# A transformer block on one core: the attention outputs' scaling one step later, and the opening in another order

## The chip, the cores and the metric

The kernel runs on one core of a Trainium2 chip. The core has a matrix engine (PE, with its weight loads shown apart as PEld), a vector engine (DVE), a scalar engine (ACT), a third elementwise engine (POOL, GpSimd in the code) and queues that start DMAs (here nearly all on SP). Each engine works through its own list of instructions in the written order and waits on semaphores for the others. [...] The metric is the device time of one execution in microseconds; lower is better. Before the change it is 2756.73 us (median of 3 runs, 2753.68 to 2758.94).

## What is computed

One transformer block with adaptive layer norm, 2048 tokens of width 576, in float32:

```
mod = silu(c) @ w_mod                       # six vectors: shift, gain, gate for both halves
h = layernorm(x) * (1 + ca) + sa
q = h @ wq                                  # 32 heads of 128
p = softmax(q @ k^T / sqrt(128))            # k, v: the last 512 rows of a cache, 16 heads, each for 2 query heads
x = x + ga * ((p @ v) @ wo)
h = layernorm(x) * (1 + cb) + sb
x = x + gb * ((silu(h @ w1) * (h @ w3)) @ w2)   # inner width 4608
```

The inputs come from a fixed seed. The kernel keeps float32 accuracy with float16 matmuls: each operand is split into a high and a low half (`high = f16(a)`, `low = f16(a - high)`), and a product takes three matmuls, high by high, high by low and low by high.

## The kernel before

Tokens are worked on in four blocks of 512. The program has an opening (to about 60 us), attention (to about 1600 us) and the MLP.

**Attention** is a sequence of 128 slots, one for a query head and a block of tokens, each about 11.6 us long and cut in four steps, t = 0 to 3. Slots overlap like a pipeline: in slot i, PE computes the scores of slot i (`scores`, tile `pss`, one tile of 128 query rows a step), the query of slot i+1 (`query`, tile `pq`), the output projection of an older pair of heads (`attend_out`, tile `pe`, six matmuls a step), and at the slot's end the attention output of slot i-1 (`values`, tile `po`, twelve matmuls, weights `v`, moving operand `ptw`). DVE takes the maximum of each score tile (`table`, L487, and a small scaling, L488); ACT takes the exponential and the row sums (`p`, L500). The weights of tiles 0 to 2 are split by ACT and POOL (`hp`) and turned by DMA into `ptw`; the last tile (t = 3) is turned by PE one slot later, and its halves are made by ACT (`turn_high`, L527) at step 1 and by DVE (`turn_low`, L552, tile `ptw`) at step 2. DVE adds the projection to the running sum at steps 1 and 3 (`acc`, L592). Row sums are inverted on DVE (`l`), written to DRAM and read back to all partitions as `r` at the end of step 2 of slot i+1 (`sums`).

`normalize(i)` (L571) is a DVE instruction that multiplies `po` by `r` into a tile `on`; ACT and POOL split `on` at step 3 (`split_on`) for the projection. `on` shares its three buffers (tag "raw") with weight loads.

**PSUM.** All eight banks are in use: tags "A", "S" and "T" have two banks each, "E" is one tile of two banks. "A" goes to `pq` and `po` by turns, "S" to `pss`, "T" to turned tiles, "E" to `pe`.

The order of the work is written out by hand: the loop over slots and steps at the end of `tile_block` issues the instructions, and `at(i, t, task)` hangs other tasks (weight preparation, statistics, MLP weights) on a step; `run(i, t)` issues them. The scheduler keeps that order on every engine and adds waits where data or buffers need them.

**The opening** normalizes block 0, forms the modulation vectors (`weigh_col`, `mod_a`, `scale_first`), splits the first head's query weights (`put_in`, `split_in`: ACT scales and converts, POOL subtracts for the low half), makes `h` of block 0 (`modulate_first`, from the turned rows in PSUM) and the first query. Then the statistics of block 1 (`norm_stats`, `norm_root`, `norm_rows`) and its `h` (`make_h`, `modulate`, five parts m = 0 to 4) come in beside slots 0 and 1. `warm` issues matmuls without use for the result.

Of the kernel before, what the change touches and what calls it, by code (L numbers as in the profile page):

```python
# [14 lines left out]
AF = mybir.ActivationFunctionType  # L15
ALU = mybir.AluOpType
# [6 lines left out]
DC = 4  # L23
# [4 lines left out]
ST = SB // P  # L28
# [13 lines left out]
SCALE = float(DH) ** -0.5  # L42
P_LOG = 15 * math.log(2.0)
Q_DOWN = 2.0**-17
# [4 lines left out]
def tile_block(  # L49
# [14 lines left out]
    nc = tc.nc  # L64
# [36 lines left out]
    gate_down, score_down = sc[:, DC + 1 : DC + 2], sc[:, DC + 2 : DC + 3]  # L101
# [88 lines left out]
    def norm_stats(b, t):  # L190
        if t == 0:
            norms[b] = odd.tile([P, ST, 2], F32, tag="mv", name="mv"), {}
        st = odd.tile([P, 2, 6], F32, tag="bst", name="bst")
        for h in range(2):
            nc.vector.bn_stats(st[:, h, :], acc[b][:, t, h * HALF : (h + 1) * HALF])
        nc.vector.bn_aggr(norms[b][0][:, t, :], st.rearrange("p a b -> p (a b)"))
# [10 lines left out]
    def warm(ps, times):  # L207
        for _ in range(times):
            nc.tensor.matmul(ps[:, :P], ones, ident, start=True, stop=True)
# [26 lines left out]
    def turn_rows(b, m, tag):  # L236

        ps = t_bank() if tag == "T" else bank(tag, "ps_n")
        for t in range(ST):
            nc.tensor.transpose(ps[:, t * P : (t + 1) * P], norms[b][1][t][:, m * P : (m + 1) * P], ident)  # L240
        return ps

    def modulate(hT, m, ps, shift, gain, on_vector=False):

        g, s = gain[:, m : m + 1], shift[:, m : m + 1]
        hf = pool.tile([P, SB], F32, tag="hf", name="hf", bufs=HF)
        high = hT[:, m if m < DC else 2 * DC, :]
        if on_vector:
            nc.vector.tensor_scalar(hf, ps, g, s, op0=ALU.mult, op1=ALU.add)
        else:  # L250
            nc.scalar.activation(hf, ps, AF.Identity, bias=s, scale=g)
        nc.gpsimd.tensor_copy(high, hf)  # L252
        if m < DC:
            nc.gpsimd.tensor_sub(hT[:, DC + m, :], hf, high)
        else:
            nc.gpsimd.tensor_sub(high[DR:], hf[DR:], high[DR:])  # L256

    def modulate_first(hT, turned, shift, gain):

        def make(m, h):  # L260
            g, s = gain[:, m : m + 1], shift[:, m : m + 1]
            if m % 2:
                nc.vector.tensor_scalar(h, turned[m], g, s, op0=ALU.mult, op1=ALU.add)
            else:
                nc.scalar.activation(h, turned[m], AF.Identity, bias=s, scale=g)

        for m in range(DC + 1):
            make(m, hT[:, m if m < DC else 2 * DC, :])
        for m in (DC, 1, 0, 3, 2):
            tag, bufs = ("p", PB) if m < DC else ("hf", HF)  # L270
            h = pool.tile([P, SB], F32, tag=tag, name="hf", bufs=bufs)
            make(m, h)
            if m < DC:
                (nc.vector if m % 2 else nc.gpsimd).tensor_sub(hT[:, DC + m, :], h, hT[:, m, :])
            else:
                nc.gpsimd.tensor_sub(hT[DR:, 2 * DC, :], h[DR:], hT[DR:, 2 * DC, :])

# [57 lines left out]
    def up_of(g, k):  # L335
        return peaks[g][:, 10 + k : 11 + k]

    def split_in(raw, g, j):

        w = pool.tile([P, 2, DC + 1, P], F16, tag="w", name="wq", bufs=WB)  # L340
        nc.scalar.activation(raw, raw, AF.Copy, scale=up_of(g, j))
        nc.scalar.copy(w[:, 0], raw)
        nc.gpsimd.tensor_sub(w[:, 1], raw, w[:, 0])
        return w

    def load_out(g):

# [103 lines left out]
    n = len(slots)  # L451
    state = [dict() for _ in range(n)]
    hT, wqs, keys, vals, wos = {}, {}, {}, {}, {}
# [95 lines left out]
    def turn_low(i, t):  # L549
        cols = slice(t * P, (t + 1) * P)  # L550
        pt = state[i]["pt"]
        nc.vector.tensor_sub(pt[:, 1, :, cols], state[i]["t"], pt[:, 0, :, cols])  # L552
# [14 lines left out]
    def normalize(i):  # L567
        st = state[i]
        po = st.pop("po")
        on = st["on"] = pool.tile([P, SB], F32, tag="raw", name="on", bufs=RB)  # L570
        nc.vector.tensor_mul(  # L571
            on.rearrange("d (t p) -> d t p", t=ST),
            po.rearrange("d (t p) -> d t p", t=ST),
            st["r"].rearrange("d p t -> d t p"),
        )
# [470 lines left out]
    vecs, gates, tasks = {}, {}, {}  # L1046

    def at(i, t, task, *args):

        tasks.setdefault((i, t), []).append((task, args))  # L1050
# [32 lines left out]
    def scale_first(ps):  # L1083

        small = odd.tile([P, 16], F32, tag="us", name="us")
        nc.vector.tensor_scalar(mod_a[:, 1], mod_a[:, 1], 1.0, None, op0=ALU.add)
        nc.vector.tensor_reduce(small[:, 0:1], mod_a, axis=AX.XY, op=ALU.max, apply_absolute_value=True)
        spread = pool.tile([P, SB], F32, tag="kv", name="spread", bufs=8)
        nc.vector.tensor_scalar(spread[:, :P], ident, small[:, 0:1], None, op0=ALU.mult)
        nc.tensor.matmul(ps[:, :P], ones, spread[:, :P], start=True, stop=True)  # L1090
        nc.vector.tensor_reduce(small[:, 2:3], ps[:, :P], axis=AX.X, op=ALU.max)
        powers(small, small[:, 2:3], 0, 1, 5, 2.0**-9)
        nc.vector.tensor_scalar(mod_a, mod_a, small[:, 10:11], None, op0=ALU.mult)
        vecs["shift", "a"], vecs["gain", "a"] = mod_a[:, 0], mod_a[:, 1]
        nc.vector.tensor_scalar(score_down, small[:, 5:6], SCALE / Q_DOWN, None, op0=ALU.mult)

    def scale_gate(kind, small, to):

# [118 lines left out]
    def put_in(u, j):  # L1217
        wqs[u, j] = split_in(wqs[u, j], uses[u][0], j)
# [123 lines left out]
    for late in range(turns):  # L1342
        number = ITEMS + 4 * late
        loader, maker, w, _ = items[number]
# [35 lines left out]
    for d in range(2 * G):  # L1380
        g = 2 * d
# [19 lines left out]
    def begin_h(b):  # L1401
        hT[b] = new_h()

    def make_h(b, m, on_vector=False):
        modulate(hT[b], m, turn_rows(b, m, "T"), vecs["shift", "a"], vecs["gain", "a"], on_vector)

    def statistics(i, b, steps):
        for t in range(ST):
# [37 lines left out]
    for c in range(3):  # L1446
        i = 117 + 3 * c
# [19 lines left out]
    for c in range(3):  # L1467
        g = 12 + 6 * c
# [60 lines left out]
    warm(junk, WARM[0])  # L1529
    take_sums(0, 0, 3)  # L1530
    powers(peaks[0], peaks[0][:, 5:10], 0, 3, 5, 2.0**-14)
    put_in(0, 0)
    for m in (0, 1, 2, 3, 4):
        weigh_col(wms[1], 1, m, True)
    keys[0] = split_k(keys[0], 0)
    put_in(0, 1)
    scale_first(junk)
    warm(junk, WARM[1])
    begin_h(0)
    modulate_first(hT[0], turned, vecs["shift", "a"], vecs["gain", "a"])  # L1540
    score_factors(0)
    keys[0] = split_k_low(*keys[0], 0)
    for t in (0, 1):
        norm_stats(1, t)
    query(0, len(QP) - 1)
    for t in (2, 3):
        norm_stats(1, t)
    norm_root(1)
    at(0, 0, norm_scale, 1)
# [6 lines left out]
        at(0, t // 2, norm_rows, 1, t)  # L1556
    at(0, 2, begin_h, 1)
    for m in range(DC + 1):
        at(*((0, 2), (0, 3), (1, -1), (1, 0), (1, 1))[m], make_h, 1, m, m % 2 == 1)
    for d, step in enumerate((5, 6, 7, 4, 5)):  # L1560
        step_at(step, weigh, 2, d)

# [1 line left out]
    for i in range(n + 2):  # L1564
        run(i, -1)
        for t in range(ST):
            if t > 1 and i < n:
                turn_away(i, t - 2)
            if t == 0 and 1 <= i <= n:
                turn_away(i - 1, 2)  # L1570
            slot, tile = (i - 1 if t == 1 else n, ST - 1)
            if 0 <= slot < n:
                turn(slot, tile)
            if i < n:
                scores(i, t)
            if 2 <= i <= n and t == 1:
                normalize(i - 2)
            if 1 <= i <= n and t == 2:
                turn_low(i - 1, ST - 1)
                if i == n:  # L1580
                    turning.close()
                    after = ctx.enter_context(tc.tile_pool(name="after", bufs=1, space=PSUM))
                    lane[1] = (E, after.tile([P, 2, 512], F32, tag="T2", name="pf"))
            if t == 3 and i + 1 < n:
                query_low(i + 1)
            if i < n:
                weights(i, t)
            if t < 3 and i < n:
                half_high(i, t)
                half_low(i, t)  # L1590
            if t == 1 and 1 <= i <= n:
                turn_high(i - 1, ST - 1)
            if 1 <= i <= n and t < 2:
                sums(i - 1, t)
            if 2 <= i <= n and t == 3:
                split_on(i - 2)
            if i + 1 < n and t < ST - 1:
                query(i + 1, t)
            if i >= m0:
                for _ in range(3 if (i, t) == (n + 1, 0) else 1):  # L1600
                    next(stream)
            for piece in outs.get((i, t), ()):
                attend_out(*piece, (i, ("total", t)))
            run(i, ("total", t))
            run(i, ("taken", t))
            run(i, t)
            if 1 <= i <= n and t == 2:
                sums(i - 1, t)
            run(i, t)
        if 1 <= i <= n:  # L1610
            values(i - 1)
        if i == n:
            normalize(n - 1)
            split_on(n - 1)
# [73 lines left out]
```

## Time and profile before

| what | before |
|---|---|
| median of 3 runs | 2756.73 us (2753.68 to 2758.94) |
| the profiled execution: time, span of its instructions | 2758.39 us, 2756.2 us |
| PE busy | 2685.1 us, 97% of the span |
| DVE, ACT, POOL busy | 1997.3, 1617.8, 1881.1 us |
| mean granted clock of PE | 0.995 |

A row of a timeline gives the start in us from the span's start, the duration, the engine, the line, the operation, the tile written and the tiles read, shapes and types, how many were merged in the row, and in brackets the idle time of the engine before it and what ended it. A row of waits reads: who waited for whom, then us in total, times, longest us. A row of grouped instructions gives line, engine, operation, tiles, shapes and count, then busy us and mean ns of one, then the idle time before them and its enders.

### The profile page before, as it was taken

The page shows a single profiled execution, that of the slowest core. Times are in us where ns is not written, and L with a number is a line of the kernel's source. Part 1 is how long each engine was busy: PE and PEld are TensorE (multiplying, and loading weights), DVE is VectorE, ACT ScalarE, POOL GpSimd, SP SyncE. Part 2 cuts the span into 40 slices and gives each one's busy share as a digit, 9 for nine tenths or more (in the row PEclk, how much of TensorE's full clock was granted, in tenths as well). Part 3 has the DMA queues.
Part 4 walks back from the last instruction along what each step waited for, and adds up shares of the span by engine and source line. Part 5 has one row for each costly group of instructions (what it writes and reads, how often), then busy time and mean ns, then how long its engine had stood idle before and what let it go on. Part 6 is the DMA issues. An engine that isn't in the chain of part 4 may idle for free. (4 is left out here: it accounts for less than half of the span.)

```text
span 2756.2 us, 44751 instructions
## 1 busy us (share of the span) xinstructions
PE 2685.1 (97%) x15406; PEld 1512.8 (55%) x15406; DVE 1997.3 (72%) x3555; ACT 1617.8 (59%) x3013; POOL 1881.1 (68%) x1748
## 2 busy tenths in 40 slices
PE   6899999999999999999999999999999999999998
PEld 3455555555555555555555555555555555555555
DVE  7877788877788787877876667777766656666666
ACT  5777778777777877777677735544443333333332
POOL 5577788888788977877669637688873465333435
PEclk8999999999999999999999999999999999999999
DMA  5778888778786887989889945656643444333332
GB/s 186 171 178 193 194 182 188 175 176 189 169 185 166 190 196 180 214 181 210 192 189 208 256 131 171 200 167 200 210 149 108 161 121 128 103 102 111 104 107 87
DMA packets 593460, 463.84 MB, mean 168 GB/s; under 512 B 442704, under 2 KB 472528, under 8 KB 592208
## 3 DMA queue, kind: packets, MB, share of 16 engines
q1 hardware_dynamic: 592944, 460.69, 65.5%
q8 instruction: 121, 1.98, 0.3%
q14 instruction: 107, 0.88, 0.1%
q10 hardware_dynamic: 288, 0.30, 0.0%
HBM read 264.19 MB, written 95.99 MB: 131 GB/s over the span
## 5 line engine op out<-in xcount | busy, mean ns | idle before, releaser
L537 POOL TENSOR_TENSOR hp<-p,hp 128x512 f16<-128x512 f32 x384 | 449.6, 1173 | 266.3 <-ACT hp L532 143.8
L500 ACT ACTIVATE p<-pss,table,factors 128x512 f32<-128x512 f32 x512 | 396.9, 775 | 354.9 <-DVE table L488 182.5
L849 PEld LDWEIGHTS <-wset 128*128 128x128 f16 x3528 | 344.5, 98 | 337.4 <-issue 4.4
L487 DVE TENSOR_REDUCE table<-pss 128x1 f32<-128x512 f32 x512 | 350.5, 685 | 206.0 <-PE pss L483 202.0
L849 PE MATMUL py<-hset,wset 128*128 128x512 f16 x2016 | 483.1, 380 | 0.0
L433 PE MATMUL pe<-o 128*128 128x288 f16 x3024 | 453.1, 286 | 10.1 <-DVE acc L592 9.6
L483 PE MATMUL pss<-k,qT 128*128 128x512 f16 x1536 | 418.8, 380 | 14.2 <-ACT p L500 10.4
L433 PEld LDWEIGHTS <-o 128*128 128x128 f16 x3072 | 300.5, 98 | 184.5 <-issue 15.7
L562 PE MATMUL po<-ptw,v 128*128 128x512 f16 x1536 | 358.2, 381 | 8.2 <-DMA ptw<-hp 4.1
L849 PE MATMUL px<-hset,wset 128*128 128x512 f16 x1512 | 361.5, 379 | 1.6 <-ACT p L500 1.6
L94 POOL TENSOR_TENSOR akv<-u,akv 128x512 f16<-128x512 f32 x141 | 165.0, 1180 | 179.2 <-ACT akv L93 171.4
L410 PE MATMUL pq<-hT,wq 128*128 128x512 f16 x1092 | 282.3, 381 | 1.8 <-POOL hT L252 1.1
L532 ACT CAST hp<-p 128x512 f16<-128x512 f32 x384 | 237.3, 618 | 13.2 <-POOL hT L256 0.6
L562 PEld LDWEIGHTS <-v 128*128 128x128 f16 x1536 | 147.8, 98 | 172.8 <-issue 16.2
L483 PEld LDWEIGHTS <-qT 128*128 128x128 f16 x1536 | 147.8, 98 | 129.2 <-issue 15.5
L934 PEld LDWEIGHTS <-akv 128*128 128x128 f16 x1728 | 169.0, 98 | 89.3 <-issue 0.8
L592 DVE SCALAR_TENSOR_TENSOR acc<-pe,factors,acc 128x576 f32<-128x576 f32 x252 | 204.6, 812 | 4.3 <-PE pe L433 4.3
L582 POOL TENSOR_TENSOR o<-on,o 128x512 f16<-128x512 f32 x128 | 150.3, 1174 | 54.0 <-ACT o L581 51.9
L410 PEld LDWEIGHTS <-wq 128*128 128x128 f16 x1092 | 107.2, 98 | 128.5 <-issue 2.9
L928 DVE SCALAR_TENSOR_TENSOR acc<-pf,table,acc 128x576 f32<-128x576 f32 x140 | 113.5, 811 | 80.8 <-PE pf L934 80.8
L1027 ACT COPY u<-py 128x512 f32<-128x512 f32 x72 | 42.2, 586 | 202.1 <-PE py L849 200.2
L1020 ACT ACTIVATE s<-s,table 128x512 f32<-128x512 f32 x72 | 52.0, 722 | 176.3 <-DVE s L1019 176.3
(246 smaller groups left out, 4793.8 us busy)
## 6 DMA issues: line engine op xcount, KB each, us to landing
wset<-wd SPq DMA_DIRECT2D x213, 320.0 KB, 3.2
r<-row SPq DMA_DIRECT2D x128, 256.0 KB, 3.9
oset<-od SPq DMA_DIRECT2D x106, 288.0 KB, 3.2
wraw<-in_w SPq DMA_DIRECT2D x36, 768.0 KB, 5.4
wd<-wmade SPq DMA_DIRECT2D x75, 320.0 KB, 3.3
wset<-wd SPq DMA_DIRECT2D x71, 160.0 KB, 2.2
w2raw<-in_w SPq DMA_DIRECT2D x19, 576.0 KB, 5.2
wd<-ring SPq DMA_DIRECT2D x33, 320.0 KB, 2.9
```

The lines of the kernel that those rows point to most:

```text
L94: eng.tensor_sub(halves[:, 1], src, halves[:, 0])
L410: nc.tensor.matmul(ps, w[:, k // 2, m, :], hT[:, DC + m if k == 1 else m, :], start=s == 0, stop=False)
L433: nc.tensor.matmul(ps[:, h, :HALF], o[:, x, rows], w[:, y, h * HALF : (h + 1) * HALF], start=first and n == 0, stop=last and n == 2,)
L483: nc.tensor.matmul(pss, q[:, x, rows], k[:, y, :], start=n == 0, stop=n == 2)
L487: nc.vector.tensor_reduce(nm[:, 0:1], pss, axis=AX.X, op=ALU.max, negate=True)
L500: nc.scalar.activation(p, pss, AF.Exp, bias=nm[:, 1:2], scale=factor, accum_out=st["l"][:, t : t + 1])
L532: nc.scalar.copy(hp[:, 0, :], state[i]["p", t])
L537: nc.gpsimd.tensor_sub(hp[:, 1, :], state[i].pop(("p", t)), hp[:, 0, :])
L562: nc.tensor.matmul(po, v[:, x, c, :], pt[:, y, c, :], start=c == 0 and n == 0, stop=c == KC - 1 and n == 2)
L592: nc.vector.scalar_tensor_tensor(a, ps[:, :, :HALF], factors[:, uses[u][0], 2:3], a, op0=ALU.mult, op1=ALU.add)
L849: nc.tensor.matmul(ps, w[:, a, :], h[:, b, :], start=start and n == 0, stop=stop and n == 6, skip_group_check=True)
L934: nc.tensor.matmul(ps[:, h, :HALF], a[:, rows], w[:, b, :], start=m == 0, stop=m == 2)
```

## The change

There are five edits.

1. `normalize(i - 2)` moves from step 1 of a slot, behind the maximum of the scores, to step 2, behind `turn_low(i - 1, 3)`.
2. POOL's two subtractions for the first head's low weight halves are issued behind `scale_first`; the score factor at the end of `scale_first` goes from DVE to POOL.
3. `modulate_first`: two parts of the first block's low half (m = 2 as well as 1 and 3) on DVE, one fewer on POOL.
4. The statistics of block 1 are issued behind the first query as a whole, where half of them stood ahead of it; the query's low half comes sooner on DVE by that.
5. `h` of block 1: DVE makes the float32 value of all five parts (before: ACT of three, DVE of two), ACT makes the high half from PSUM itself (before: POOL copied it from the float32 value), POOL only subtracts; three of the five parts are hung one step earlier.

```diff
-        nc.gpsimd.tensor_copy(high, hf)
+            nc.gpsimd.tensor_copy(high, hf)
...
-        if on_vector:
+        if early:
             nc.vector.tensor_scalar(hf, ps, g, s, op0=ALU.mult, op1=ALU.add)
+            nc.scalar.activation(high, ps, AF.Identity, bias=s, scale=g)
...
-                (nc.vector if m % 2 else nc.gpsimd).tensor_sub(hT[:, DC + m, :], h, hT[:, m, :])
+                (nc.vector if m else nc.gpsimd).tensor_sub(hT[:, DC + m, :], h, hT[:, m, :])
...
-    def split_in(raw, g, j):
+    def split_in(raw, g, j, low=True):
         w = pool.tile([P, 2, DC + 1, P], F16, tag="w", name="wq", bufs=WB)
         nc.scalar.activation(raw, raw, AF.Copy, scale=up_of(g, j))
         nc.scalar.copy(w[:, 0], raw)
+        if low:
+            split_in_low(w, raw)
+        return w
+
+    def split_in_low(w, raw):
         nc.gpsimd.tensor_sub(w[:, 1], raw, w[:, 0])
-        return w
...
-        nc.vector.tensor_scalar(score_down, small[:, 5:6], SCALE / Q_DOWN, None, op0=ALU.mult)
+        nc.gpsimd.tensor_scalar(score_down, small[:, 5:6], SCALE / Q_DOWN, None, op0=ALU.mult)
...
-    put_in(0, 0)
+    raws = [wqs[0, j] for j in range(2)]
+    wqs[0, 0] = split_in(raws[0], 0, 0, False)
...
-    put_in(0, 1)
+    wqs[0, 1] = split_in(raws[1], 0, 1, False)
     scale_first(junk)
+    for j in range(2):
+        split_in_low(wqs[0, j], raws[j])
...
-    for t in (0, 1):
-        norm_stats(1, t)
     query(0, len(QP) - 1)
-    for t in (2, 3):
+    for t in range(ST):
         norm_stats(1, t)
...
-        at(*((0, 2), (0, 3), (1, -1), (1, 0), (1, 1))[m], make_h, 1, m, m % 2 == 1)
+        at(*((0, 2), (0, 3), (0, 3), (1, -1), (1, 0))[m], make_h, 1, m, True)
...
-            if 2 <= i <= n and t == 1:
-                normalize(i - 2)
             if 1 <= i <= n and t == 2:
                 turn_low(i - 1, ST - 1)
+                if i > 1:
+                    normalize(i - 2)
```

The changed kernel's lines are numbered five or six higher around these places (L571 becomes L576, L552 L557, L562 L567).

How it moves instructions, in three places. First DVE in slot 32, steps 1 to 3; before:

```order
L487 TENSOR_REDUCE table_223<-pss_5004 128x1
L488 TENSOR_SCALAR table_223<-table_223,factors_101 128x1
L571 TENSOR_TENSOR on_5010<-po_4956,r_4930 128x512
L592 SCALAR_TENSOR_TENSOR acc1_90<-pe_76,factors_101,acc1_90 128x576
L1141 COPY table_223<-pe_76 128x2
L1145 TENSOR_SCALAR table_223<-table_223 128x1
L1146 TENSOR_SCALAR table_223<-table_223 128x1
L1147 RECIPROCAL table_223<-table_223 128x1
L487 TENSOR_REDUCE table_223<-pss_5042 128x1
L488 TENSOR_SCALAR table_223<-table_223,factors_101 128x1
L552 TENSOR_TENSOR ptw_4900<-pt_4999,ptw_4900 128x4x128
L487 TENSOR_REDUCE table_223<-pss_5073 128x1
```

The same place now:

```order
L492 TENSOR_REDUCE table_223<-pss_5004 128x1
L493 TENSOR_SCALAR table_223<-table_223,factors_101 128x1
L597 SCALAR_TENSOR_TENSOR acc1_90<-pe_76,factors_101,acc1_90 128x576
L1146 COPY table_223<-pe_76 128x2
L1150 TENSOR_SCALAR table_223<-table_223 128x1
L1151 TENSOR_SCALAR table_223<-table_223 128x1
L1152 RECIPROCAL table_223<-table_223 128x1
L492 TENSOR_REDUCE table_223<-pss_5040 128x1
L493 TENSOR_SCALAR table_223<-table_223,factors_101 128x1
L557 TENSOR_TENSOR ptw_4898<-pt_4999,ptw_4898 128x4x128
L576 TENSOR_TENSOR on_5047<-po_4956,r_4930 128x512
L492 TENSOR_REDUCE table_223<-pss_5073 128x1
```

`on` has gone from ahead of `acc` to behind `ptw`; everything else stands as it did. Second, PE at the end of the same slot, the last projection matmul and the first of `po`, with what each waits for; before:

```order
L433 MATMUL pe_76<-o_4237,o_4942 128x288
L562 LDWEIGHTS v_3791 [waits DMAHW7_49,DMAHW4_49,DMAHW1_49]
L562 MATMUL po_5098<-ptw_4900,v_3791 128x512 [waits Activation_49]
L562 LDWEIGHTS v_3791
L562 MATMUL po_5098<-ptw_4900,v_3791 128x512
L562 LDWEIGHTS v_3791
L562 MATMUL po_5098<-ptw_4900,v_3791 128x512 [waits DVE_49]
```

and now:

```order
L438 MATMUL pe_76<-o_4237,o_4942 128x288
L567 LDWEIGHTS v_3791 [waits DMAHW4_49,DMAHW7_49,DMAHW1_49,DVE_49]
L567 MATMUL po_5098<-ptw_4898,v_3791 128x512 [waits Activation_49]
L567 LDWEIGHTS v_3791
L567 MATMUL po_5098<-ptw_4898,v_3791 128x512
L567 LDWEIGHTS v_3791
L567 MATMUL po_5098<-ptw_4898,v_3791 128x512
```

The one wait for DVE has gone from the third matmul to the first weight load. `po_5098` takes the "A" bank of `po_4956`, the tile that `on_5047` reads. Third, POOL in the opening, from the modulation's last product to the end of block 1's `h`; before:

```order
L130 TENSOR_TENSOR wmr<-wmr,gate_b 128x576
L343 TENSOR_TENSOR wq<-wraw,wq 128x640 x2
L276 TENSOR_TENSOR hT<-hf,hT 64x512
L274 TENSOR_TENSOR hT<-hf,hT 128x512 x2
L537 TENSOR_TENSOR hp<-p,hp 128x512
L233 COPY xn<-xn 128x64 x2
```

and now:

```order
L130 TENSOR_TENSOR wmr<-wmr,gate_b 128x576
L1100 TENSOR_SCALAR sc<-us 128x1
L349 TENSOR_TENSOR wq<-wraw,wq 128x640 x2
L277 TENSOR_TENSOR hT<-hf,hT 64x512
L275 TENSOR_TENSOR hT<-hf,hT 128x512
L542 TENSOR_TENSOR hp<-p,hp 128x512
```

The score factor (`sc`), which waits for DVE's scaling, stands ahead of the two weight halves, and one subtraction of `hT` is gone from POOL.

More of the change, by code (lines that the diff above doesn't have):

```diff
@@ L241, in turn_rows, with modulate @@
         return ps
-    def modulate(hT, m, ps, shift, gain, on_vector=False):
+    def modulate(hT, m, ps, shift, gain, early=False):
         g, s = gain[:, m : m + 1], shift[:, m : m + 1]
@@ L1402, in begin_h, with make_h @@
         hT[b] = new_h()
[L1404 to L1405 removed]
+    def make_h(b, m, early=False):
+        modulate(hT[b], m, turn_rows(b, m, "T"), vecs["shift", "a"], vecs["gain", "a"], early)
     def statistics(i, b, steps):
```

## The prediction

> **What bounds the kernel now.** I read first how busy each engine is in stretches of the span (start and end, length, then busy us and count of PE, weight loads, DVE, ACT and POOL, then PE's granted clock, DMA share and GB/s), then the waits, then the rows of single slots in order of time.
>
> ```profile
> 200.00:400.00 200.00, 196.57 (x1121) 109.73 (x1120) 151.79 (x308) 149.58 (x291) 160.08 (x155) 1.00 0.83 194
> ...
> 1600.00:1800.00 200.00, 200.00 (x1186) 115.66 (x1184) 144.55 (x228) 91.70 (x148) 123.43 (x117) 1.00 0.50 163
> ```
>
> PE sets the time. In attention (to about 1600 us) it is busy 196.57 of 200 us, in the MLP all of it. So whatever the edit to attention does is bounded below: it can give back only the few waits that PE has there, while a new wait of PE adds to the span in full. These are the large groups of PE's waits between 100 and 1600 us, and, from the waits of DVE, what stops the instruction that is moved (`on`, L571) and the one it is moved behind (`ptw`, L552):
>
> ```profile
> PE pe L433 <- DVE acc L592: 9.6, 10, 2.4
> PE pss L483 <- ACT p L500: 6.8, 13, 1.7
> PE po L562 <- DVE ptw L552: 2.4, 6, 0.7
> ...
> DVE ptw L552 <- ACT ptw L527: 25.1, 19, 3.3
> DVE on L571 <- POOL o L582: 8.7, 9, 2.5
> DVE on L571 <- DMA r<-row: 5.5, 4, 2.9
> ```
>
> **The move of `on`.** At step 1 of a slot, DVE multiplies the attention output of two slots ago by the reciprocal sums, 128x512 from PSUM, 1.09 us:
>
> ```profile
> L571 DVE TENSOR_TENSOR on<-po,r 128x512 f32<-128x512 f32 x128 | 139.1, 1087 | 17.2 <-POOL o L582 8.7 <-DMA r<-row 5.5 <-PE po L562 1.8
> L552 DVE TENSOR_TENSOR ptw<-pt,ptw 128x512 f16<-128x512 f32 x128 | 87.6, 684 | 27.2 <-ACT ptw L527 25.1 <-DMA wraw<-in_w 1.6
> ```
>
> What it gives back: where `on` waits (for `r`, or for POOL to free its buffer), `acc` behind it is late, and PE, which needs `acc` to free its one E bank, stops. The worst case, after the wait of 2.9 for `r`:
>
> ```profile
> 582.80 0.81 DVE L592 SCALAR_TENSOR_TENSOR acc<-pe,factors,acc 128x576 f32<-128x576 f32 x1
> 583.67 0.90 PE L433 MATMUL pe<-o 128*128 128x288 f16 x6 [2.43 <-DVE acc L592]
> ```
>
> PE goes on 0.06 us after `acc` ends (582.80 + 0.81 = 583.61); I use this 0.06 below. Of the ten waits on `acc`, nine follow an `on` that waited so. With `on` out of the way they go: **-9 us**.
>
> What it costs: `on` frees the PSUM bank that the `po` of the slot before takes at the end of the same slot (tag "A", two banks, `pq` and `po` by turns). In the new order, PE's first weight load for `po` has a wait for DVE, and what it needs from DVE is `on`; before, `po`'s third matmul waited for `ptw`. So `po` starts 1.05 us or so after the end of `ptw` at the earliest, where `ptw` only had to be there for the third matmul. A usual slot, by DVE and PE in order of time:
>
> ```profile
> 436.67 1.08 DVE L571 TENSOR_TENSOR on<-po,r 128x512 f32<-128x512 f32 x1
> 436.69 0.90 PE L433 MATMUL pe<-o 128*128 128x288 f16 x6
> 437.67 0.82 DVE L592 SCALAR_TENSOR_TENSOR acc<-pe,factors,acc 128x576 f32<-128x576 f32 x1
> ...
> 439.93 0.69 DVE L552 TENSOR_TENSOR ptw<-pt,ptw 128x512 f16<-128x512 f32 x1
> ...
> 441.10 1.24 PE L562 MATMUL po<-ptw,v 128*128 128x512 f16 x5
> ```
>
> Here `on` lies beside PE's output-weight matmuls, which end at 437.59; `acc` needs these and starts at 437.67 whether `on` is ahead of it or not. So taking `on` away makes nothing earlier: `ptw` still ends at 440.62. A next DVE instruction begins up to 0.1 before the last one's end (`on` to `acc` above), so `on` would run 440.52 to 441.60, and `po` could start at 441.66, not 441.10: PE waits 0.56. Slots with nothing between `acc` and the maximum just escape:
>
> ```profile
> 569.81 0.68 DVE L552 TENSOR_TENSOR ptw<-pt,ptw 128x512 f16<-128x512 f32 x1
> 571.61 2.75 PE L562 MATMUL po<-ptw,v 128*128 128x512 f16 x12
> ```
>
> `on` would end at 571.47, and PE waits for nothing. And where `ptw` itself waits for ACT's half, PE pays most:
>
> ```profile
> 513.06 0.69 DVE L552 TENSOR_TENSOR ptw<-pt,ptw 128x512 f16<-128x512 f32 x1 [0.91 <-ACT ptw L527]
> 513.32 2.80 PE L562 MATMUL po<-ptw,v 128*128 128x512 f16 x12
> ```
>
> `on` 513.65 to 514.75, `po` at 514.8 in place of 513.32: 1.5 us.
>
> I laid out all 125 slots from 2 to 126 in this way, each by its own rows (DVE's durations kept, `acc` not ahead of PE's matmuls, `ptw` not ahead of ACT, an `on` that waits for `r` or POOL not ahead of that). From `ptw`'s end to `po`'s start there are now -0.20, 0.41 and 1.02 us at the quartiles, where 1.05 are wanted unless `ptw` comes earlier; it seldom does, since in 95 slots `acc` starts within 0.2 us of the end of PE's matmuls. The sums of PE's new waits: 34 slots none; 66 slots behind DVE work 52 us together (0.8 each); 19 slots with a late ACT 24 us; the six first ones (2 to 7) 7 us. Not all of it stays, since PE's wait in one slot lets DVE and ACT catch up for the next. Where `acc` waits for PE in its own slot nothing is caught up; of the 52 I keep **45**. Of the 19, six follow directly on another one with ACT busy throughout, and are covered by the first one's wait (-7.6), and others follow a slot that waits too: of 24 I keep **9**, of the first 7 us **4**. Against it, PE's waits for `ptw` above are contained in the new ones (**-2.4**), and ACT gains on PE in some slots where `pss` waited for it (**-2**). Bounds of this term with the -9: at most 52 + 24 + 7 - 11 = +72; at least, if only the excess over the slot before counted, about half of 45 + 9 + 4, less 13: +15.
>
> **The opening.** POOL's two weight halves now lie behind the scaling of the modulation. They hit DVE now:
>
> ```profile
> 18.83 3.88 POOL L343 TENSOR_TENSOR wq<-wraw,wq 128x640 f16<-128x640 f32 x2 [2.37 <-ACT wq L342]
> 18.84 0.76 DVE L128 SCALAR_TENSOR_TENSOR wc<-wc,gate_b 128x576 f32<-128x576 f32 x1
> 19.51 1.95 DVE L128 SCALAR_TENSOR_TENSOR wmr<-wmr,gate_b 128x576 f32<-128x576 f32 x1
> 21.50 1.23 DVE L1086 TENSOR_SCALAR mod_a<-mod_a 128x5 f32<-128x5 f32 x1
> 24.62 0.15 DVE L295 TENSOR_SCALAR us<-us 128x1 int32<-128x1 int32 x1
> ```
>
> Under POOL's two, DVE's like operations take 1.95 for 0.76 and 1.23 for 0.15: 2.3 us on the chain to the first query. In the new place the two lie beside DVE's subtractions for the first `h`, of which DVE has one more (m = 2, about 0.7). [...]
>
> The query's low half sooner takes away a wait of 1.33:
>
> ```profile
> 34.64 0.64 DVE L473 SCALAR_TENSOR_TENSOR qT<-pe,qT 128x512 f16<-128x512 f32 x1
> 35.34 0.39 PE L483 MATMUL pss<-k,qT 128*128 128x512 f16 x1 [1.33 <-DVE qT L473]
> ```
>
> but the statistics of block 1 behind it end no sooner, and DVE is what the next 20 us hang on (below). The second block's `h`: POOL loses five copies and ACT converts from PSUM; what PE can win is the wait for the last part, 2.94.
>
> ```profile
> 57.74 1.62 POOL L256 TENSOR_TENSOR hT<-hf,hT 64x512 f16<-64x512 f32 x1
> 59.42 0.75 PE L414 MATMUL pq<-hT,wq 128*128 128x512 f16 x2 [2.94 <-POOL hT L256]
> ...
> 47.90 0.81 DVE L249 TENSOR_SCALAR hf<-pt,mod_a 128x512 f32<-128x512 f32 x1
> ...
> 48.00:56.00 8.00, 6.18 (x31) 3.22 (x30) 7.30 (x11) 5.89 (x11) 6.99 (x8) 0.91 0.29 91
> 56.00:64.00 8.00, 5.06 (x18) 1.90 (x16) 4.69 (x14) 3.92 (x8) 5.79 (x5) 0.79 0.21 46
> ```
>
> All five `hf` are DVE's now, three more of 0.81: 2.4 us on an engine busy 7.3 of 8 us. ACT's two more conversions fit (5.89 of 8). And a turn of `xn` stands a step earlier in PE's queue; it needs a bank that DVE's `hf` frees, and now has the first scores of slot 1 behind it. The score factor, now POOL's, costs a row of 0.15 ahead of work that had to wait anyway. Sum: -2.3 + 2.4 + 0.7 - 2.9 and something of the 1.3: **-2.5**; bounds -10 (all of 2.3 + 1.3 + 2.9 + 1.8 for the smaller waits on `hT` and the half clock behind them) and +4 (nothing but DVE's additions).
>
> **Sum.** +45 + 9 + 4 - 9 - 2.4 - 2 - 2.5 = +42 on the profiled execution's 2758.4 us; the median of the three runs is 1.7 lower, so 2757 + 42 = 2799.
>
> **Rivals.** (a) *The bank wait is hidden, and the relief counts* (12%): DVE or ACT run ahead once `on` no longer stops DVE, `ptw` comes early enough, and PE keeps its pace. For it speaks that `on` waits 14 us in all for `r` and POOL; against it that `acc`, ahead of `ptw`, starts on PE's own matmuls. It decides for faster if `ptw` ends 1.05 us ahead of `po` in all but a tenth of the slots: 2757 - 9 - 2.5 = 2745. (b) *Only slots with a late ACT pay* (5%), the others being met by slack that I do not see: +9 + 4 - 9 - 2.4 - 2.5, no change, 2756. (c) *The full price* (20%): nothing is caught up, +72: about 2827. (d) *The clock* (4%): PE's new waits lower its granted clock.
>
> ```profile
> 72.00:76.00 4.00, 1.79 (x8) 0.52 (x7) 3.93 (x8) 2.44 (x5) 2.00 (x2) 1.00 0.52 131
> ```
>
> PE busy 1.79 of 4 us kept full clock here, and after the 2.94 us wait it was 0.79 over 8 us, some 1.7 us lost. If ten of the longest waits did that: 17 more, 2816. [...]
>
> **How the numbers follow.** My own case, slower by about 42 us, has 59%, and with it 2770 to 2820 as its own range. Slower are also (c) and (d): 83%. (a) is faster, 12%, (b) the same, 5%; a difference under 0.2% (5.5 us) can't be told from none in a measurement of this kernel. The range 2765 to 2830 leaves out (a) and (b).
>
> **What would show it.** A new row among PE's waits, `po` L567 for DVE `on`, of some 50 to 70 us in 60 to 90 times, the one for `acc` near 1 us, and `on`'s own waits nearly gone; PE busy 192 to 194 of 200 us in attention; no change after 1600 us. In the opening DVE's row for `wmr` near 0.76 and no 2.94 at the last part of `hT`. I am wrong if `ptw` ends earlier against `po` than now, or if PE's wait for `on` is under 20 us in sum.

## The result and the profile after

| what | before | after |
|---|---|---|
| median | 2756.73 us | 2806.19 us (5 runs, 2800.74 to 2808.52) |
| ratio to before, 95% interval | 1 | 1.0178, 1.0164 to 1.0193 |
| the profiled execution: time, span | 2758.39, 2756.2 us | 2800.74, 2798.9 us |
| PE busy | 2685.1 us, 97% | 2686.0 us, 96% |
| mean granted clock of PE | 0.995 | 0.996 |

The change makes the kernel 1.8% slower, 49 us on the medians. PE has the same work, 2686 us, in a longer span, at the same clock: it waits. Stretches of the changed kernel, columns as before (start and end, length, busy us and count of PE, weight loads, DVE, ACT, POOL, then clock, DMA share, GB/s):

```profile
200.00:400.00 200.00, 190.09 (x1082) 105.69 (x1081) 146.28 (x299) 143.96 (x279) 155.62 (x149) 1.00 0.80 188
...
600.00:800.00 200.00, 189.31 (x1086) 105.20 (x1085) 154.38 (x313) 152.89 (x294) 162.48 (x155) 1.00 0.76 177
...
1800.00:2000.00 200.00, 200.00 (x1173) 113.86 (x1171) 143.16 (x204) 98.55 (x165) 162.44 (x145) 1.00 0.58 192
```

In attention PE is busy 190 of 200 us where it was 196.6; in the MLP nothing has changed. The first maximum of slot 4 comes 0.8 us later than before, that of slot 127 43.9 later, and the program's end 42.7 later: all of the loss lies in attention, spread over it (7.4 us by slot 24, 23.9 by slot 64, 41.8 by slot 112).

Which of PE's groups wait, from 100 to 1560 us: first three groups of the kernel before, then the same three of the changed one (busy us, mean ns of one, then the idle time before the group and what ended it):

```profile
L433 PE MATMUL pe<-o 128*128 128x288 f16 x2904 | 435.6, 286 | 10.1 <-DVE acc L592 9.6 <-DVE us L315 0.2
L483 PE MATMUL pss<-k,qT 128*128 128x512 f16 x1452 | 393.9, 379 | 8.7 <-ACT p L500 6.8 <-DVE qT L473 0.7 <-ACT qT L467 0.4
L562 PE MATMUL po<-ptw,v 128*128 128x512 f16 x1458 | 337.9, 379 | 7.2 <-DMA ptw<-hp 4.1 <-DVE ptw L552 2.4
```

```profile
L438 PE MATMUL pe<-o 128*128 128x288 f16 x2820 | 422.3, 286 | 0.0
L488 PE MATMUL pss<-k,qT 128*128 128x512 f16 x1410 | 381.4, 379 | 3.0 <-ACT p L505 2.0 <-DVE qT L478 0.9
L567 PE MATMUL po<-ptw,v 128*128 128x512 f16 x1416 | 325.7, 380 | 60.4 <-ACT hp L537 33.1 <-DVE on L576 26.8 <-DMA ptw<-hp 0.3
```

`po` has gone from 7.2 us of waiting to 60.4, `pe` from 10.1 to nothing, `pss` from 8.7 to 3.0. Half of the 60.4 is put down to ACT's `hp`. That name misleads: `po`'s first matmul has a wait for ACT, but the weight load ahead of it has the wait for DVE, and the waits of the weight loads, from 100 to 1640 us, name `on` (and in 82 of the 84 slots with a gap of PE over 0.15 us ahead of `po`, `po` starts within 0.12 us of the end of `on`):

```profile
PEld L567 <- DVE on L576: 78.0, 81, 2.4
```

The rows of slot 32, of which the prediction showed the old ones (436.67 to 441.10), in the changed kernel:

```profile
449.72 0.82 DVE L597 SCALAR_TENSOR_TENSOR acc<-pe,factors,acc 128x576 f32<-128x576 f32 x1 [0.91 <-PE pe L1140]
...
451.98 0.69 DVE L557 TENSOR_TENSOR ptw<-pt,ptw 128x512 f16<-128x512 f32 x1
452.59 1.06 DVE L576 TENSOR_TENSOR on<-po,r 128x512 f32<-128x512 f32 x1
...
452.42 0.90 PE L438 MATMUL pe<-o 128*128 128x288 f16 x6
453.71 2.76 PE L567 MATMUL po<-ptw,v 128*128 128x512 f16 x12 [0.39 <-DVE on L576]
```

DVE now stands idle for 0.91 ahead of `acc`, where `on` used to lie, and `po` starts 0.06 us after `on` ends (452.59 + 1.06 = 453.65). Over the slots 2 to 126 the distance from `on`'s end to `po`'s start is 0.06, 0.06 and 0.10 us at the quartiles; before, 3.29, 3.32 and 3.38. Taken slot by slot from the last matmul ahead of `po` to its first, PE's gaps add up to 66.6 us, 84 of them over 0.15; before, 4.5 us and 5.

### The profile page after: what moved, and what is told of

Read it like the earlier page. It is cut to its first block, busy times and chain, and to the rows that moved or that the text cites. A ratio compares the mean times of both kernels' runs of the same rounds, so it can differ in the third digit from the quotient of the medians.

```text
span 2798.9 us, 44864 instructions
## 1 busy us (share of the span) xinstructions
PE 2686.0 (96%) x15406; PEld 1507.7 (54%) x15406; DVE 1999.7 (71%) x3558; ACT 1625.2 (58%) x3015; POOL 1878.2 (67%) x1743
## 4 chain that ended last, share of the span: by engine, by line
PE 50%; DVE 2%; issue 1%; ACT 1%; DMA 0%; POOL 0%; SPq 0%; ACTq 0%; DVEq 0%; POOLq 0%
PE py L854 15%; PE px L854 11%; PE pf L939 7%; PE pe L939 6%; PE po L567 3%; PE pe L438 2%; PE pq L415 2%; PE pss L488 2%; PE pt L528 0%; DVE acc L597 0%; ACT hp L537 0%; DVE table L492 0%; DVE acc L950 0%; PE pf L438 0%; PE pq L419 0%
## 5 line engine op out<-in xcount | busy, mean ns | idle before, releaser
L567 PE MATMUL po<-ptw,v 128*128 128x512 f16 x1536 | 356.7, 382 | 67.0 <-ACT hp L537 34.0
L567 PEld LDWEIGHTS <-v 128*128 128x128 f16 x1536 | 142.9, 98 | 245.6 <-DVE on L576 82.8
L537 ACT CAST hp<-p 128x512 f16<-128x512 f32 x384 | 237.3, 618 | 13.7 <-POOL hT L257 0.6
```

The costliest lines, as they stand in the source:

```text
L537: nc.scalar.copy(hp[:, 0, :], state[i]["p", t])
L567: nc.tensor.matmul(po, v[:, x, c, :], pt[:, y, c, :], start=c == 0 and n == 0, stop=c == KC - 1 and n == 2)
```

## The experiments

Each ratio is to the kernel before in the same job, with its 95% interval. The table is for looking up; what was expected and what follows is told below.

| run | what it is | median us | ratio to before |
|---|---|---|---|
| after | the whole change | 2806.19 | 1.0178 (1.0164 to 1.0193) |
| e1 | the move of `on` alone | 2807.14 | 1.0177 (1.0160 to 1.0194) |
| e2 | the opening edits alone | 2757.53 | 0.9991 (0.9980 to 1.0002) |
| e3 | the change, `on` at step 2 ahead of `ptw` | 2767.62 | 1.0035 (1.0022 to 1.0048) |
| e4 | the change, `po` never in the bank that `on` reads | 2762.61 | 1.0015 (1.0005 to 1.0026) |
| e5 | the change, half of `on` at step 1 | 2775.86 | 1.0064 (1.0050 to 1.0077) |
| e6 | as e4, `on` at step 3 | 2781.53 | 1.0083 (1.0069 to 1.0097) |
| e12 | as e4, `on` at step 1 | 2756.39 | 0.9990 (0.9981 to 0.9999) |
| e10 | the opening edits but that to the query, `on` at step 1 | 2756.69 | 0.9983 (0.9975 to 0.9992) |
| e11 | as e10, `on` at step 2 ahead of `ptw` in 11 slots | 2754.00 | 0.9972 (0.9963 to 0.9981) |

### The two halves of the change

e1 is the kernel before with edit 1 alone:

```diff
-            if 2 <= i <= n and t == 1:
-                normalize(i - 2)
             if 1 <= i <= n and t == 2:
                 turn_low(i - 1, ST - 1)
+                if i > 1:
+                    normalize(i - 2)
```

> The kernel before with the move of `on` alone, none of the opening edits. Theory (po's first weight load waits for `on`, which frees its bank): 2799 to 2808, the changed kernel's time with the opening's few us given back. Rival (the opening edits are what costs): 2755 to 2759.

e2 is the changed kernel with these lines put back, so edits 2 to 5 alone.

> The changed kernel with `on` back at step 1, so the opening edits alone. Theory: 2750 to 2757, forecast 2754, since the opening was put at -2.5 with bounds -10 and +4. Rival (the opening edits cost): above 2760.

Measured: 1.0177 (2807.14 us) and 0.9991 (2757.53 us, half a microsecond above the theory's range; the kernel before stands at 2759.72 in that job). The move is the whole loss; the opening edits cost nothing that can be seen and may give about 2 us, with an interval that includes none. The move's price is 49 us by e1 and, from e2 to the whole change, 1.0178 / 0.9991 = 1.0187, 51 us; each is good to about 5 us.

### Is it the bank, or the place in DVE's queue?

In e3 `on` stands at the same step, but ahead of `ptw`:

```diff
+            if 2 <= i <= n and t == 2:
+                normalize(i - 2)
             if 1 <= i <= n and t == 2:
                 turn_low(i - 1, ST - 1)
-                if i > 1:
-                    normalize(i - 2)
```

> The changed kernel with `on` at step 2 but ahead of `ptw` in place of behind it. Theory: `on` is then done when po's first weight load wants its bank, and `ptw`, 1.05 us later than in the kernel before, is wanted only by po's third matmul, 0.43 us after the first; of each slot's wait about 0.45 goes: 2775 to 2792, forecast 2785. Rival (it is not the bank: two DVE instructions between the second and the third maximum delay the maximum of the last tile, and ACT with it): the third maximum is as late as in the changed kernel, so 2800 to 2810.

Measured: 1.0035, 2767.62 us. The rival's 2800 is far off; so is the theory's 2785, on the good side. What the forecast left out is in the waits of DVE, here of e2 and then of e3, 100 to 1640 us:

```profile
DVE ptw L557 <- ACT ptw L532: 23.9, 21, 3.0
```

```profile
DVE ptw L557 <- ACT ptw L532: 7.6, 12, 1.7
```

Where ACT's half of the turned tile is late, DVE stands idle ahead of `ptw`, and `on` now fills that time for nothing: 16 us less of waiting on DVE. PE's rows bear it out. In the 22 slots in which e2's `ptw` waits over 0.15 us for ACT, PE loses nothing at `po` in e3 against e2, where it loses 16 us in the whole change; in the other 103 slots it loses 30 us, against which the relief for `acc` stands.

e4 takes the bank away and leaves `on` behind `ptw`. The two "A" and the two "T" banks are put in one list; `pq`, `po` and the turned tiles each take the bank that has been free longest, and give it back behind its last reader:

```diff
-            st["q"] = bank("A", "pq") if i else E[:, 0, :]
+            st["q"] = take(lambda: bank("A", "pq")) if i else E[:, 0, :]
...
-        ps = st["t"] = t_bank().rearrange("p (j n) -> p j n", j=KC)
+        st["bank"] = take(new_t)
+        ps = st["t"] = st["bank"].rearrange("p (j n) -> p j n", j=KC)
...
-        po = bank("A", "po")
+        po = take(lambda: bank("A", "po"))
```

> The changed kernel, `on` behind `ptw` as there, but the four banks of the tags A and T are given out by the program to pq, po and the turned tiles in the order in which they come free, from slot 2 to slot 124. po then takes a bank that was free long before, and PE's wait for DVE is at po's third matmul again. Theory: the whole price of the move goes, and what it relieved (the waits for acc behind a late `on`) stays: 2743 to 2757, forecast 2747. Rival (the place of `on` in DVE's queue costs, whatever the bank): 2795 or more.

Measured: 1.0015, 2762.61 us, above the theory's range and far below the rival's. Of the move's 1.87% the bank was 1.0178 / 1.0015 = 1.0163, 45 us. The gaps of PE ahead of `po` add up to 8.1 us, against 66.6. But the kernel isn't below e2, as the theory had it: something of the place is left. The scores and the waits of their weight loads for the query's low half (`qT`), from 100 to 1560 us, in e4:

```profile
L507 PE MATMUL pss<-k,qT 128*128 128x512 f16 x1446 | 394.5, 379 | 21.3 <-ACT p L524 9.6 <-DVE qT L497 9.6 <-ACT qT L489 1.3
...
PEld L507 <- DVE qT L497: 25.4, 44, 1.9
```

In DVE's order the query's low half stands behind the third maximum, and both stand behind `on`. e12 is e4 with `on` back at step 1:

> The four banks given out as they come free, with `on` at step 1 as in the kernel before; with all opening edits. It splits the 0.24 percent by which the four-bank kernel with `on` behind `ptw` stands above the opening edits alone. Theory (the place of `on` costs it, by the query's low half that comes later on DVE; the banks cost nothing): ratio 0.9985 to 0.9997, as the opening edits alone, and PE's waits for the low half back near 8 us. Rival (the hand-made order of the banks costs): ratio 1.0005 or more.

Measured: 0.9990, as e2, and

```profile
L507 PE MATMUL pss<-k,qT 128*128 128x512 f16 x1455 | 394.8, 379 | 8.5 <-ACT p L524 6.8 <-DVE qT L497 0.7 <-ACT qT L489 0.4
...
PEld L507 <- DVE qT L497: 7.8, 19, 0.8
```

So the list of banks by itself costs and gives nothing that can be seen, and the place of `on` behind `ptw` costs 1.0015 / 0.9990 = 1.0025, 7 us (between 3 and 11, from the two intervals), in place of a gain: the waits for `acc` are gone in e4 too, but the later `qT` costs more. PE's starts say the same: from the first maximum of slot 2 to that of slot 127, e4 takes 7.9 us longer than e12; the scores come 16.9 us later in sum, `pe` comes 13.7 sooner, and 4.7 lie elsewhere. With the bank in the way this can't be seen, since PE's wait at `po` gives DVE the time (in the changed kernel PE waits 0.9 us for `qT`). So a bank for `po` that nothing still reads is worth 45 us where the reader is late (e4 against the whole change), and nothing that can be seen where it is early (e12, 0.9990, against e2, 0.9991).

e5 halves the instruction that `po` waits for: the first two of four token tiles at step 1, the others behind `ptw`.

```diff
+            if 2 <= i <= n and t == 1:
+                normalize(i - 2, (0,))
             if 1 <= i <= n and t == 2:
                 turn_low(i - 1, ST - 1)
                 if i > 1:
-                    normalize(i - 2)
+                    normalize(i - 2, (1,))
```

> The changed kernel with `on` cut in two along the tokens: the first half at step 1 (the old place), the second behind `ptw` (the new place), so the instruction behind `ptw` takes some 0.55 us in place of 1.09. Theory (po waits for ptw's end plus the duration of what stands behind it): in the rows of before po starts -0.20, 0.41 and 1.02 us after ptw's end at the quartiles, so the wait falls from 1.25, 0.64 and 0.03 to some 0.7, 0.1 and 0, about 40 percent of the price: 2770 to 2788, forecast 2777. Rival (the wait is for a semaphore or a queue place, and goes with the number of instructions, not their length): 2800 or more.

Measured: 1.0064, 2775.86 us, 1.1 us below the forecast. The groups of `on` (whole run) and `po` (100 to 1560 us):

```profile
L579 DVE TENSOR_TENSOR on<-po,r 128x256 f32<-128x256 f32 x254 | 154.9, 610 | 12.8 <-POOL o L590 6.4 <-DMA r<-row 6.3
```

```profile
L567 PE MATMUL po<-ptw,v 128*128 128x512 f16 x1435 | 330.0, 380 | 33.1 <-DVE on L579 30.7 <-ACT p L505 1.4
```

The time behind `ptw` falls from 1.09 to 0.61, and `po`'s waits from 60.4 to 33.1. It is the length that counts.

### A later place

e6 keeps e4's banks and puts `on` at step 3, behind the query's low half.

> As the kernel with the four banks given out as they come free, but `on` at step 3, behind the low half of the query (slots 2 to 124). There nothing of the next scores stands behind it, and PE is about to run po's twelve matmuls, 4.5 us. Theory: in the four-bank kernel `on` behind ptw took away the waits for acc (9.6) but made the query's low half late (PE's waits for it 36 against 8); here the first gain stays and the second loss goes: 2742 to 2752, forecast 2747, faster than both. Rival (the hand-made order of the banks itself costs, or acc of step 3 behind `on` is late for PE): 2757 or more.

Measured: 1.0083, slower than e4 and than e12, where the theory had it faster than both; the rival holds. (The theory's "4.5 us" for `po`'s twelve matmuls, about twelve times the 379 ns of the group's row, was also wrong; the rows have 2.75 for the twelve.) The wait for `qT` is gone (0.7 us), but PE's scores wait 18.9 us for ACT's `p` (9.6 in e4), and 5.5 us of waits for `acc` are back: step 3 has little room on DVE or ACT. DVE and PE at the end of slot 31:

```profile
433.67 1.06 DVE L600 TENSOR_TENSOR on<-po,r 128x512 f32<-128x512 f32 x1
434.65 0.81 DVE L621 SCALAR_TENSOR_TENSOR acc<-pe,factors,acc 128x576 f32<-128x576 f32 x1
435.38 0.74 DVE L389 SCALAR_TENSOR_TENSOR v<-kvraw,us,v 128x512 f16<-128x512 f32 x1
436.04 0.95 DVE L1155 TENSOR_REDUCE peak_cols<-wraw 128x1 bf16<-128x768 f32 x1
436.90 0.68 DVE L511 TENSOR_REDUCE table<-pss 128x1 f32<-128x512 f32 x1
...
433.83 0.81 PE L507 MATMUL pss<-k,qT 128*128 128x512 f16 x3
```

The scores of the next slot end at 434.64, and their maximum starts at 436.90, behind `on`, `acc` and hung work. ACT's split of `on` follows at the same step and stops ACT's queue:

```profile
ACT o L610 <- DVE on L600: 58.6, 101, 1.0
```

### The opening, edit by edit

These three ran once each and are read from their traces: when the first maximum of a slot starts, against the kernel before (37.3, 65.6 and 80.1 us for slots 0, 2 and 3). A part of such a shift only tells when the first loads came: e1 has the opening of the kernel before, and its slot 0 stands at -1.0. So the table also counts the shifts from the start of DVE's `wmr` row (19.51 in the kernel before), which no edit moves. Counted so, e1 still has -0.3 and -0.5 at slots 0 and 2; finer than that the numbers are not.

| run | shift of slots 0, 2, 3, us | counted from `wmr` |
|---|---|---|
| e2, all opening edits | -1.0, -2.8, -2.7 | -0.8, -2.7, -2.6 |
| e7, edit 5 | -0.7, -2.2, -2.1 | 0.0, -1.6, -1.5 |
| e8, edit 2 | -1.4, -1.4, -1.4 | -1.1, -1.1, -1.1 |
| e9, edit 4 | +0.5, +0.8, +1.5 | +0.6, +0.9, +1.6 |
| e10, all but edit 4 | -1.9, -2.8, -2.7 | -1.6, -2.5, -2.4 |

e7, edit 5 alone (the second block's `h`): 

> The kernel before with the edit to the second block's h alone. By the maximum of the first score tile of slots 0, 2 and 3 against before (the changed order without the move of `on`: -1.0, -2.8, -2.7 us). Theory (the wait of 2.94 for the last part of hT goes, and DVE's three more hf cost 2.4): 0, -1 to +1, -1 to +1. Rival (this edit is what the opening gains): 0, -2, -2 or more.

Measured: 0.0, -1.6, -1.5 from `wmr`, between the theory and the rival. The wait of 2.94 for the last part is gone, as are those of 0.75 and 1.07 ahead of it; PE's turning of `xn` waits 4.4 us for ACT's new conversion, where it waited 2.1 for ACT before. The three more `hf` on DVE cost nothing that can be seen. Of the three edits tried alone this one gains most.

e8, edit 2 alone (weight halves later): 

> The kernel before with the weight halves behind the modulation's scaling and the score factor on POOL, nothing else. Theory (DVE's wmr and mod_a run free of POOL, 2.3 us on the chain to the first query): slot 0 -2, slot 2 -2, slot 3 -2. Rival (the two meet DVE's subtractions for h instead, and the first query's low halves come later): slot 0 -1 or less gained, slot 2 and 3 within 1.

Measured: -1.1 from `wmr` at all three slots, little over half of the theory's -2. DVE and POOL:

```profile
19.20 0.76 DVE L128 SCALAR_TENSOR_TENSOR wmr<-wmr,gate_b 128x576 f32<-128x576 f32 x1
...
22.56 1.46 DVE L1097 TENSOR_SCALAR mod_a<-mod_a,us 128x10 f32<-128x10 f32 x1
...
22.60 2.75 POOL L348 TENSOR_TENSOR wq<-wraw,wq 128x640 f16<-128x640 f32 x2
...
28.68 1.11 DVE L319 TENSOR_SCALAR factors<-us,sc 128x2 f32<-128x2 f32 x1
29.70 1.72 DVE L390 SCALAR_TENSOR_TENSOR k<-kvraw,us,k 128x512 f16<-128x512 f32 x1
```

The 2.3 us are given back (`wmr` 0.76 for 1.95, and 0.17 for the row of 1.23), but the scaling of the modulation, 0.23 before, takes 1.46 beside POOL's halves: by these rows 1.0 us is left.

e9, edit 4 alone (the query's low half ahead of all statistics): 

> The kernel before with block 1's statistics behind the first query, nothing else. Theory (the wait of 1.33 of the first scores goes, but the statistics, on which the next 20 us hang, end no sooner): PE's wait for the low half gone; slot 0 -0.5 to +1.5, slot 2 and 3 within 0.7. Rival (it is worth its wait): slots 2 and 3 -1.3.

Measured: +0.6, +0.9, +1.6 from `wmr`: a loss by itself, larger than the theory's 0.7 at slots 2 and 3.

```profile
33.26 0.69 DVE L473 SCALAR_TENSOR_TENSOR qT<-pe,qT 128x512 f16<-128x512 f32 x1 [0.55 <-ACT qT L467]
...
37.81 0.69 DVE L487 TENSOR_REDUCE table<-pss 128x1 f32<-128x512 f32 x1
```

DVE now waits 0.55 for ACT's half of the query, which two of the statistics had filled, and all four stand ahead of the first maximum.

### A version below both

In the kept traces with `on` at step 1, its waits for `r` and POOL fall into the same slots (ten of the eleven below in every one of them), so they can be avoided there alone. e10 is the opening without edit 4, `on` at step 1; e11 adds

```diff
-            if 2 <= i <= n and t == 1:
+            late = i in (36, 37, 44, 57, 68, 69, 76, 84, 93, 121, 124)
+            if 2 <= i <= n and t == (2 if late else 1):
                 normalize(i - 2)
```

> The opening edits without the one that puts block 1's statistics behind the first query, and `on` at step 1. Alone that edit put slot 3's first maximum 1.5 us later, while the edit to h alone put it 2.1 sooner and the weight halves 1.4 sooner. If these add up: about 4 to 5 us below the kernel before at slot 3, and 2752 to 2755 in time, ratio 0.998 to 0.9985, against 0.9991 with the edit. Rival (they don't add, since the query's low half is late only while DVE is free of the other work): slot 3 at -2.7 as with the edit, ratio 0.999 to 1.000.

> As that kernel, but in the 11 slots in which `on` waits at step 1 for r or for POOL (36, 37, 44, 57, 68, 69, 76, 84, 93, 121, 124) it goes to step 2, ahead of `ptw`; elsewhere it stays. Theory (PE's stops behind a late acc, some 9.5 us in these slots, are the move's only gain, and ahead of `ptw` the price is at most 0.6 us a slot): PE's waits for acc near 1 us, 3 to 8 us below the kernel with `on` at step 1 everywhere: 2746 to 2751, ratio 0.995 to 0.9975. Rival (PE's stop there is made up in the slots that follow, or comes back at `po`): within 1.5 us of it.

Measured: 0.9983 and 0.9972. e10 stands at slot 3 where e2 does (-2.7), as its rival had it: there edit 4 costs nothing beside the others. The times don't decide it: 0.9983 lies in the range of the theory, that the gains add, and its interval reaches into the rival's and overlaps e2's. e11 is faster than the kernel before, 0.28% with its interval clear of 1. From 100 to 1560 us, of e11:

```profile
L438 PE MATMUL pe<-o 128*128 128x288 f16 x2921 | 437.4, 286 | 1.0 <-DVE acc L597 0.4
L567 PE MATMUL po<-ptw,v 128*128 128x512 f16 x1454 | 337.1, 379 | 10.1 <-DMA ptw<-hp 4.4 <-DVE ptw L557 2.5 <-DVE on L576 1.7
```

`pe`'s waits are gone (12.1 in e10's profile), and `on` costs 1.7 at `po`. In the kept traces the way from the first maximum of slot 4 to that of slot 127 is 1474.7 us in e11, and 1478.7 to 1484.0 in the seven kernels with `on` at step 1 throughout (before, e2, e7 to e10, e12), so attention did get shorter. How much e11 gains on e10 in all is not settled: 2.7 us between medians, with intervals that overlap.

## Why the prediction was right, point by point

**The mechanism** held: the wait moved to `po`'s first weight load, and the three slots that the prediction worked out came as it said, if they are counted as it counted, by how much later `po` starts. In the kernel before, PE's rows of slot 32 are:

```profile
440.37 0.90 PE L433 MATMUL pe<-o 128*128 128x288 f16 x6
441.10 2.75 PE L562 MATMUL po<-ptw,v 128*128 128x512 f16 x12
```

`po` waits for nothing here and starts 0.17 us ahead of the (modelled) end of `pe` (440.37 + 0.90 = 441.27), so a wait delays it by about that much more than the idle time in brackets (0.39 in the changed kernel). `po` started 0.73 us behind `pe` here and starts 1.29 behind it in the changed kernel (452.42 to 453.71): 0.56 later, with 0.56 forecast. In slot 38, with a late ACT, it is 1.46 (1.5 forecast), in slot 43 nothing (nothing). These two, in the changed kernel:

```profile
526.84 0.69 DVE L557 TENSOR_TENSOR ptw<-pt,ptw 128x512 f16<-128x512 f32 x1 [1.26 <-ACT ptw L532]
527.45 1.05 DVE L576 TENSOR_TENSOR on<-po,r 128x512 f32<-128x512 f32 x1
528.56 2.76 PE L567 MATMUL po<-ptw,v 128*128 128x512 f16 x12 [1.29 <-DVE on L576]
...
587.81 1.08 DVE L576 TENSOR_TENSOR on<-po,r 128x512 f32<-128x512 f32 x1
589.06 1.24 PE L567 MATMUL po<-ptw,v 128*128 128x512 f16 x5
```

**The sum** came out near, but in part by luck. Between the first maximum of slot 2 and that of slot 127, PE's groups start later or sooner by these sums:

| term, us | forecast | before to e1 | e2 to the change |
|---|---|---|---|
| first matmul of `po` | 45 + 9 + 4 = +58 | +76.5 | +76.1 |
| the other matmuls of `po` (the old wait for `ptw`) | -2.4 | -6.9 | -6.9 |
| `pe` (the waits for `acc`) | -9 | -14.0 | -14.6 |
| `pss` | -2 | -9.4 | -8.6 |
| the whole way, all else with it | +44.6 | +47.4 | +47.4 |

The new waits were put 18 us too low and the relief 17 us too low; the two errors nearly cancel.

**The keeping of waits** (45 of 52, 9 of 24, 4 of 7) is the step that was mis-sized: in e1 the three kinds of slots paid 54.5, 14.9 and 7.1. Where DVE's own work makes `ptw` late, and in the first slots, nothing was caught up. Only behind a late ACT was less than the raw sum paid, 14.9 of 24, and 7.6 of that difference the prediction had itself worked out, for slots that follow directly on another. What PE's new wait gives the other engines shows up as relief instead: PE hardly waits any more for `acc`, for `ptw` and for ACT's `p`.

**The time.** On the profiled execution the forecast was 2758.4 + 42 = 2800.4, and its successor has 2800.74. That close an agreement is chance: the five executions of the changed kernel spread from 2800.74 to 2808.52, and the profiled one is the fastest. The medians lie 1.7 below the one and 5.5 above the other, and that is where the 7 us between 2799 and 2806 come from. By the medians the move costs 49 to 51 us (to about 5 us), by the traces 47.4 up to slot 127, not 44.6. What lies between these is within the noise: the stretch from there to the end, nearly all MLP, which no edit touches, takes 1180.7 to 1187.4 us in the kept traces.

**The relief** was taken for a gain that stays (-9). `pe` keeps it in e4, where PE doesn't wait at `po`, but there the later query half costs more than it, 7 us net (e4 against e12): a place in the queue that the prediction didn't price, since behind `on` it named the wait of `po`, not `qT`.

**The opening**: -2.5 forecast, 0.9991 measured, which is -2.5 within an interval of -5.5 to +0.6. The interval includes none, and e2's slot 3 has -2.6. The total was right, its parts were not, so that is luck too. Weight halves: -2.3 forecast, -1.1 by e8. The second block's `h`: +2.4 - 2.9 forecast, -1.5 by e7; the smaller waits on `hT` went too, and DVE's additions can't be seen. The query sooner: nothing to -1.3 forecast, +1.6 alone by e9, and about nothing at slot 3 beside the others by e10. The subtraction of m = 2 on DVE: +0.7 forecast; no run has this edit alone. The row itself takes 1.64 us in the changed kernel (the longer of the two in the first row below), but POOL's second subtraction is gone, and two DVE rows are short that took 1.11 and 1.72 in e8 above:

```profile
27.64 2.53 DVE L275 TENSOR_TENSOR hT<-hf,hT 128x512 f16<-128x512 f32 x2
...
30.10 0.28 DVE L320 TENSOR_SCALAR factors<-us,sc 128x2 f32<-128x2 f32 x1
30.29 0.74 DVE L391 SCALAR_TENSOR_TENSOR k<-kvraw,us,k 128x512 f16<-128x512 f32 x1
```

Counted from DVE's first `hT` row (23.92 here, 24.06 in e8), `k` ends after 7.11 us, in e8 after 7.36: about -0.3, not +0.7.

**The rivals.** (a) and (b), the bank wait hidden or paid only with a late ACT, fall with e1 and the gaps in 84 slots. (c), the full price: 76 of the 83 us of raw waits were paid, so on the side of the cost it was nearer than the prediction's own case; its 2827 failed because the relief was 30 us where it took 11 off. (d), the clock: 1.00 in every stretch of attention from 200 us on.

**The signs that it named.** The new row stands among PE's waits, though under two names: `po` for `on` 26.8 us in 36 times and, put down to ACT's `hp`, 33.1 in 43, together 59.9 in 79 (50 to 70 in 60 to 90 forecast). PE busy 192 to 194 of 200 us was a little high (189.3 to 193.9 from 200 to 1600 us); the waits for `acc` and those of `on` itself are gone, the MLP is unchanged, DVE's `wmr` is short again, and no wait of 2.94 stands at the last part of `hT`. One of the two signs of being wrong could not have told: from `ptw`'s end to `po`'s start there are now 1.04, 1.05 and 1.11 us at the quartiles, so `ptw` does end earlier against `po`, only because `po` waits.

## What to carry to other kernels

An instruction that reads a PSUM bank out belongs where its engine would otherwise wait: ahead of an `acc` that waits for PE's matmuls anyway, `on` cost PE nothing but in the few slots in which it waited itself (9.6 us of waits for `acc`, nine of the ten behind such an `on`), and 3.8 us later it cost 1.8%, since `pq` and `po`, which take turns in two banks here, have one bank each. Before a reader is moved, ask which matmul takes its bank next, how long before it the reader now ends, and what stands behind the reader in the new place: here the bank was some 45 us and the query's half behind it some 7. A forecast that adds a cost and a relief can be right by two errors of one size, so both are worth measuring. The wait that recurred in known slots was best removed in those slots alone (e11, 0.9972, the lowest ratio of the runs).

## What was not expected of the hardware

A DVE instruction over 10 columns was held up beside POOL for as long as a large one. The scaling of 128x10 takes 1.46 us in the changed kernel and in e8, where POOL's halves lie beside it, and 0.23 in the kernel before, where they have ended: 1.23 more. `wmr`, of 128x576, takes 1.95 beside the halves and 0.76 without them: 1.19 more. In e8 POOL's first subtraction (1.40 us of the 2.75 for two) starts 0.04 us after the scaling, and the scaling ends 0.02 us after that subtraction. The prediction and e8's rival had the halves beside DVE's subtractions for `h` in the new place; in e8 the halves end at 25.35, and the first of these subtractions starts at 26.34 and takes 0.69. Of the 2.3 us, 1.1 is left in e8. The rows show how long the two engines' instructions take beside each other; why DVE's lasts as long as POOL's is not shown.
